# Lightning attention and a feed-forward in float32: attention steps reordered by matmul form, weights converted without GpSimd, leaky ReLU as one ScalarE operation, decay read as a Toeplitz matrix from memory

## The chip, the cores and the metric

The kernel runs on one core of one Trainium2 chip. The metric is device microseconds of one execution, the median of several runs. A core has TensorE (matmuls; PE in the profile, its weight loads PEld), VectorE (DVE), ScalarE (ACT), GpSimd (POOL) and SyncE (SP, which here only issues loads). Each takes its own instructions in order and waits for the others by semaphores. TensorE's clock is granted at one of two levels, 1.2 or 2.4 GHz; the profile shows the granted share, 1.00 being the higher.

## The reference

Batch 4, 8 heads, 768 positions, head size 64. `q` and `k`, `v` and `lam` are float32; the weights `moe_w_in` (512 x 2048) and `moe_w_out` (2048 x 512) are float64.

```python
for b in range(nb):                       # blocks of 64 positions
    intra = einsum('bhic,bhjc->bhij', qb, kb) * Dmask    # lam^(i-j) for i >= j, else 0
    intra = einsum('bhij,bhjd->bhid', intra, vb)
    inter = einsum('bhid,bhde->bhie', qb * lam_pow, kv_state)   # lam^(i+1)
    out[:, :, sl] = intra + inter
    kv_state = lam**64 * kv_state + einsum('bhsd,bhse->bhde', kb * rev_pow, vb)
x = out.transpose(0, 2, 1, 3).reshape(3072, 512)
h = x @ w_in
result = np.maximum(0.01 * h, h) @ w_out      # (3072, 512), float32
```

## The kernel before

The attention runs in 24 chunks of 128 positions, six for each batch, all heads at once, heads in pairs (one on partitions 0-63, one on 64-127). A chunk has three stages. `stage_a` loads the chunk three ahead, transposes k and q through PSUM tile `pt` (one buffer; VectorE copies kT out, ScalarE qT) and lets GpSimd make `qsT` = qT times lam^(i+1) (`pow_q`) and `kd` = k times its decay. `stage_b` forms the scores `ps` (products of 64 rows, in two halves of the array), which VectorE multiplies by `decay` into `sc`, and the state update `pu` (128 rows by 128 columns), from which VectorE makes the new `state` (L291). `stage_c` forms the output `po`: for every pair of heads one state product (L301, 128 rows by 128 columns) and then two value products (L304, 64 columns each); ScalarE copies it into `xT`. In the first chunk of a batch there is no state product, in the last no state update.

The feed-forward runs in six groups of four chunks: 16 `up` units (4 matmuls of 512 columns each, then `small` = 0.01 h on ScalarE and the maximum on VectorE, giving `gT`) and 4 `down` units (16 matmuls each). In float32 every matmul is two records in the profile, a transpose one. The stages of the next group's chunks are emitted between the units, and a scheduler then orders each engine's queue by its own model.

The weights come as 32 blocks of float64 (128 partitions x 512), loaded three ahead by SyncE, and `convert_w` rounds them on the chip: GpSimd clamps (L135) and squares (L136) the high words, VectorE works on the bits (L137, L138, L140 to L142), and GpSimd adds the low part (L143). Block n of the first 16 serves the up unit n; the last 16 serve the down units. They are converted during the first group.

The powers of lam for `decay` are made on VectorE by more than fifty small instructions (L175 to L226), `pow_q` on GpSimd.

Of the kernel before, what the change touches and what calls it, by code (L numbers as in the profile page):

```python
# [12 lines left out]
The weights come as float64, whose bits the chip rounds to float32 once, before their first use.  # L13
"""
# [28 lines left out]
def kernel(  # L43
# [35 lines left out]
    pp_t = ctx.enter_context(tc.tile_pool(name="pp_t", bufs=1, space=PS))  # L79
    pp_s = ctx.enter_context(tc.tile_pool(name="pp_s", bufs=2, space=PS))  # L80
    pp_o = ctx.enter_context(tc.tile_pool(name="pp_o", bufs=1, space=PS))
    pp_h = ctx.enter_context(tc.tile_pool(name="pp_h", bufs=2, space=PS))
    pp_y = ctx.enter_context(tc.tile_pool(name="pp_y", bufs=2, space=PS))

# [1 line left out]
    lam_b = const.tile([P, H], F32, name="lam_b")  # L86
    nc.scalar.dma_start(out=lam_b, in_=lam.partition_broadcast(P))
# [17 lines left out]
    def load_w(n):  # L105
        """The float64 bits of the n-th block: w_in for 128 features, then w_out for as many."""
# [7 lines left out]
    HI_MIN = _float_of(0x38100000)  # L114

    def convert_w(n):
        """The n-th block rounded to float32.

        A float64 is (-1)^s 2^(e-1023) (1 + m 2^-52), its high word s, e (11 bits) and the upper 20
        bits of m. While 2^-126 <= |x| < 2^128, e's upper four bits are 0111 or 1000, and the  # L120
        float32 of s, e and these 20 bits has s and e's top bit at its bits 31 and 30 and the low 27
        bits of the high word at 29-3. The low word, times 2^(e-1023-52), is then added in float32.
        Before that, magnitudes past float32 are brought down to its largest ones; what is below
        2^-126 becomes 0. Seen as float32s, the high words stand in the order of the float64s, and the
        squares of those that are left neither overflow nor underflow at these two bounds.
        """
# [11 lines left out]
        nc.vector.scalar_tensor_tensor(out=wi, in0=ti, scalar=-0x40000000, in1=wi,  # L138
                                       op0=ALU.bitwise_and, op1=ALU.bitwise_or)
# [22 lines left out]
    NR, NI = 16, C // 16 + 1  # L162
    NE = NR + NI + 1
    NB = 7
    ex = const.tile([P, NE], I32, name="ex")
    nc.gpsimd.iota(ex[:, 0:NR], pattern=[[1, NR]], base=0, channel_multiplier=-1)
    nc.gpsimd.iota(ex[:, NR:NR + NI], pattern=[[16, NI]], base=-1, channel_multiplier=-1)
    nc.gpsimd.iota(ex[:, NE - 1:NE], pattern=[[1, 1]], base=C - 1, channel_multiplier=-1)
    ir_i = const.tile([P, NR], I32, name="ir_i")
    nc.gpsimd.iota(ir_i, pattern=[[1, NR]], base=0, channel_multiplier=0)  # L170
    jr_i = const.tile([P, 1], I32, name="jr_i")
    nc.gpsimd.iota(jr_i, pattern=[[1, 1]], base=0, channel_multiplier=1)

    e_lo, e_hi = ex[:, 0:NR], ex[:, NR:NR + NI]
    nc.vector.tensor_scalar(e_lo, e_lo, 15, None, op0=ALU.bitwise_and)  # L175
    nc.vector.tensor_scalar(e_hi, e_hi, -16, None, op0=ALU.bitwise_and)
    nc.vector.tensor_scalar(jr_i, jr_i, 15, None, op0=ALU.bitwise_and)
    hi_ok = const.tile([P, NI], F32, name="hi_ok")
    nc.vector.tensor_scalar(hi_ok, e_hi, 0.0, None, op0=ALU.is_ge)
    nc.vector.tensor_scalar(e_hi, e_hi, 0.0, None, op0=ALU.max)  # L180

    ir_f = const.tile([P, NR], F32, name="ir_f")
    nc.vector.tensor_copy(ir_f, ir_i)
    jr_f = const.tile([P, 1], F32, name="jr_f")
    nc.vector.tensor_copy(jr_f, jr_i)
    same = const.tile([P, 2, NR], F32, name="same")
    nc.vector.tensor_scalar(same[:, 0, :], ir_f, jr_f[:, 0:1], None, op0=ALU.is_ge)
    nc.vector.tensor_scalar(same[:, 1, :], ir_f, jr_f[:, 0:1], None, op0=ALU.is_lt)

    bit_i = const.tile([P, NB, NE], I32, name="bit_i")  # L190
    for n in range(NB):
        nc.vector.tensor_scalar(bit_i[:, n, :], ex, n, 1, op0=ALU.arith_shift_right, op1=ALU.bitwise_and)
    bit = const.tile([P, NB, NE], F32, name="bit")
    nc.vector.tensor_copy(bit, bit_i)
    nbit = const.tile([P, NB, NE], F32, name="nbit")
    nc.vector.tensor_scalar(nbit, bit, -1.0, 1.0, op0=ALU.mult, op1=ALU.add)

    sq = const.tile([P, NB, H], F32, name="sq")
    nc.vector.tensor_copy(sq[:, 0, :], lam_b)
    for n in range(1, NB):  # L200
        nc.vector.tensor_tensor(sq[:, n, :], sq[:, n - 1, :], sq[:, n - 1, :], op=ALU.mult)

    # pw[j, h, e] = lam_h ^ ex[j, e]: the product of lam^(2^n) over the exponent's bits
    pw = const.tile([P, H, NE], F32, name="pw")
    for n in range(NB):
        f = pw if n == 0 else at2.tile([P, H, NE], F32, name="pf", tag="pf")
        nc.vector.tensor_tensor(f, _bc(bit[:, n, :], 1, H), _bc(sq[:, n, :], 2, NE), op=ALU.mult)
        nc.vector.tensor_tensor(f, f, _bc(nbit[:, n, :], 1, H), op=ALU.add)
        if n:
            nc.vector.tensor_tensor(pw, pw, f, op=ALU.mult)  # L210
    pw_hi = const.tile([P, H, NI], F32, name="pw_hi")
    nc.vector.tensor_tensor(pw_hi, pw[:, :, NR:NR + NI], _bc(hi_ok, 1, H), op=ALU.mult)
    pw_lo = const.tile([P, 2, H, NR], F32, name="pw_lo")
    for x in range(2):
        nc.vector.tensor_tensor(pw_lo[:, x], pw[:, :, 0:NR], _bc(same[:, x, :], 1, H), op=ALU.mult)
# [3 lines left out]
    decay = const.tile([P, 2, HP, C], F32, name="decay")  # L219
    for hi in range(2):  # L220
        terms = (decay[:, hi].rearrange("p a (b r) -> p a b r", r=NR),
                 at2.tile([P, HP, C], F32, name="dterm", tag="sc").rearrange("p a (b r) -> p a b r", r=NR))
        for x, dst in enumerate(terms):
# [178 lines left out]
```

## Time and profile before

| | |
|---|---|
| time, median of 3 runs | 898.42 us (898.36 to 903.91) |
| span of the profiled execution, first to last instruction | 898.1 us |
| TensorE matmul busy | 829.5 us, 2816 records |
| VectorE busy | 286.1 us, 518 instructions |
| GpSimd busy | 171.7 us, 159 instructions |
| ScalarE busy | 100.7 us, 169 instructions |
| feed-forward matmuls L322, L332 | 344.2 and 339.7 us busy, 768 records each |

The profiled execution has no time of its own beside its span, which is 0.3 us under the median. Busy times of matmuls overlap their neighbours (the mean record of 0.60 us starts every 0.43 us), so what a group of matmuls costs is read from the chain of waits, where every piece ends where the next begins.

### The profile page before, as it was taken

Reading aid. Unit: us, or ns where it says so; the run is one execution under the profiler, and the core shown is the slowest. Engines: PE = TensorE matmul, PEld = TensorE weight load, DVE = VectorE, ACT = ScalarE, POOL = GpSimd, SP = SyncE. Lnnn points to the kernel's source line nnn. Section 1 sums busy time; section 2 is a strip of 40 time slices with the busy share of each in tenths; the row PEclk is TensorE's granted clock in tenths of the full one; section 3 lists DMA queues with packets and bytes.
Section 4 is the critical chain, followed back from the end, with each engine's and each line's share of the span. In section 5 each row is a group of like instructions: output and inputs, shape, how many; then the busy total and the mean of one; then the engine's idle time right before and its main releaser. Section 6 shows DMA issues by size and latency. Waiting matters only on the chain.

```text
span 898.1 us, 7069 instructions
## 1 busy us (share of the span) xinstructions
PE 829.5 (92%) x2816; PEld 408.3 (45%) x2816; DVE 286.1 (32%) x518; ACT 100.7 (11%) x169; POOL 171.7 (19%) x159
## 2 busy tenths in 40 slices
PE   4885678759999999999999999999999999999998
PEld 3652234324455444454445454444454444444443
DVE  8789999991022220022211022111032110012000
ACT  1110101001011100011200011100011100011000
POOL 5377877771010000010010010010010000000000
PEclk9977988979999999999999999999999999999999
DMA  9354434321110102110101110111100000000000
GB/s 230 84 132 127 130 111 135 99 78 47 35 47 12 35 1 58 36 47 12 36 28 32 36 47 12 36 34 26 47 1 1 0 12 12 23 1 0 0 24 23
DMA packets 89265, 42.41 MB, mean 47 GB/s; under 512 B 75920, under 2 KB 84112, under 8 KB 89232
## 3 DMA queue, kind: packets, MB, share of 16 engines
q1 hardware_dynamic: 85632, 35.66, 15.8%
q10 hardware_dynamic: 3600, 6.30, 1.9%
q8 instruction: 22, 0.36, 0.2%
q14 instruction: 11, 0.09, 0.0%
HBM read 35.66 MB, written 6.29 MB: 47 GB/s over the span
## 4 chain that ended last, share of the span: by engine, by line
PE 79%; POOL 12%; issue 4%; DVE 4%; DMA 1%; ACT 0%; POOLq 0%; DVEq 0%
PE py L332 35%; PE ph L322 31%; POOL raw L136 4%; PE po L304 3%; PE ps L273 3%; POOL w_out L143 3%; PE po L301 3%; POOL wt L135 3%; POOL w_in L143 2%; PE pu L282 2%; PE pt L258 2%; DMA raw<-in_moe_w_in_dram 0%; DVE wt L141 0%; POOL kd L266 0%; DMA lam_b<-in_lam_dram 0%
## 5 line engine op out<-in xcount | busy, mean ns | idle before, releaser
L322 PE MATMUL ph<-xT,w_in 128*128 128x512 f32 x768 | 344.2, 602 | 16.1 <-DVE gT L326 15.3
L332 PE MATMUL py<-w_out,gT 128*128 128x512 f32 x768 | 339.7, 598 | 10.4 <-POOL w_out L143 10.4
L322 PEld LDWEIGHTS ph<-xT,w_in 128*128 128x128 f32 x768 | 144.5, 193 | 188.6 <-issue 177.6
L332 PEld LDWEIGHTS py<-w_out,gT 128*128 128x128 f32 x768 | 144.1, 191 | 183.6 <-issue 167.9
L326 DVE TENSOR_TENSOR gT<-ph,small 128x512 f32<-128x512 f32 x96 | 66.1, 689 | 240.2 <-ACT small L324 240.1
L324 ACT ACTIVATE small<-ph 128x512 f32<-128x512 f32 x96 | 57.3, 597 | 325.4 <-PE ph L322 317.1
L277 DVE TENSOR_TENSOR sc<-ps,decay 128x512 f32<-128x512 f32 x48 | 31.3, 684 | 187.4 <-PE ps L273 187.3
L266 POOL TENSOR_TENSOR kd<-k,pw 128x512 f32<-128x512 f32 x20 | 22.0, 1102 | 306.5 <-PE pu L282 224.9
L263 POOL TENSOR_TENSOR qsT<-qT,pow_q 128x512 f32<-128x512 f32 x20 | 26.0, 1299 | 217.0 <-ACT qT L260 217.0
L301 PE MATMUL po<-qsT,state 128*128 128x128 f32 x160 | 40.3, 336 | 14.7 <-DVE state L291 14.6
L260 DVE COPY kT<-pt 128x512 f32<-128x512 f32 x24 | 16.6, 690 | 109.5 <-PE pt L258 109.4
L335 ACT COPY osb<-py 128x512 f32<-128x512 f32 x24 | 14.0, 585 | 309.3 <-PE py L332 309.3
L304 PE MATMUL po<-sc,v 128*64 128x128 f32 x384 | 43.8, 315 | 5.2 <-DVE sc L277 5.2
L301 PEld LDWEIGHTS po<-qsT,state 128*128 128x128 f32 x160 | 27.1, 203 | 34.0 <-issue 18.8
L136 POOL TENSOR_TENSOR raw<-wt 128x512 f32<-128x512 f32 x32 | 41.3, 1291 | 2.5
L273 PE MATMUL ps<-qT,kT 64*128 64x128 f32 x384 | 34.2, 312 | 7.6 <-DVE sc L277 5.6
L273 PEld LDWEIGHTS ps<-qT,kT 64*128 64x128 f32 x384 | 28.5, 210 | 20.4 <-issue 11.3
L142 DVE SCALAR_TENSOR_TENSOR wt<-raw,wt 128x512 f32<-128x512 uint32 x32 | 30.5, 954 | 0.0
L304 PEld LDWEIGHTS po<-sc,v 128*64 128x64 f32 x384 | 21.3, 145 | 19.5 <-DVE sc L277 5.6
L143 POOL TENSOR_TENSOR w_out<-w_out,wt 128x512 f32<-128x512 f32 x16 | 26.0, 1624 | 18.3 <-DVE wt L142 18.3
L291 DVE SCALAR_TENSOR_TENSOR state<-state,pow_q,pu 64x64 f32<-64x64 f32 x128 | 28.3, 279 | 2.2 <-PE pu L282 1.6
L135 POOL TENSOR_SCALAR wt<-raw 128x512 f32<-128x512 f32 x32 | 27.6, 862 | 2.4
(57 smaller groups left out, 296.8 us busy)
## 6 DMA issues: line engine op xcount, KB each, us to landing
raw<-in_moe_w_in_dram SPq DMA_DIRECT2D x16, 512.0 KB, 3.8
raw<-in_moe_w_out_dram SPq DMA_DIRECT2D x16, 512.0 KB, 3.3
q<-in_q_dram SPq DMA_DIRECT2D x24, 256.0 KB, 3.8
k<-in_k_dram SPq DMA_DIRECT2D x24, 256.0 KB, 3.8
v<-in_v_dram SPq DMA_DIRECT2D x24, 256.0 KB, 3.7
out_dram<-osb ACTq DMA_DIRECT2D x24, 256.0 KB, 2.0
lam_b<-in_lam_dram ACTq DMA_DIRECT2D x1, 4.0 KB, 3.3
```

The source lines that it names most:

```text
L135: nc.gpsimd.tensor_scalar(t, hi, HI_MAX, -HI_MAX, op0=ALU.min, op1=ALU.max)
L136: nc.gpsimd.tensor_tensor(hi, t, t, op=ALU.mult)
L142: nc.vector.scalar_tensor_tensor(out=t, in0=lo, scalar=2.0 ** -52, in1=t, op0=ALU.mult, op1=ALU.mult)
L143: nc.gpsimd.tensor_tensor(w, w, t, op=ALU.add)
L273: nc.tensor.matmul(ps[hi][:, hp, :], lhsT=kT[c][HALF[hi], hp, :], rhs=qT[c][HALF[hi], hp, :], start=True, stop=True)
L277: nc.vector.tensor_tensor(sc[c][:, hi], ps[hi], decay[:, hi], op=ALU.mult)
L301: nc.tensor.matmul(po[:, hp, :], lhsT=state[(c - 1) % NST][:, hp, :], rhs=qsT[c][:, hp, :], start=True, stop=False)
L304: nc.tensor.matmul(po[HALF[hi], hp, :], lhsT=tv[:, 2 * hp + hi, :], rhs=sc[c][:, hi, hp, :], start=first, stop=True)
L322: nc.tensor.matmul(ph, lhsT=w_in_sb[f][:, ko, :], rhs=xT[g][:, ko, :], start=(ko == 0), stop=(ko == KO - 1))
L324: nc.scalar.activation(out=small, in_=ph, func=AF.Copy, bias=0.0, scale=0.01)
L326: nc.vector.tensor_tensor(t, ph, small, op=ALU.max)
L332: nc.tensor.matmul(py, lhsT=gT[f][:, ms * P:(ms + 1) * P], rhs=w_out_sb[f], start=(f == 0), stop=(f == FO - 1))
```

## The change

1. The three stages become one function `step(s)` for chunks a = s, b = s - 1 and c = s - 2, whose matmuls are emitted in groups: transposes of k, all state products of c, transposes of q, scores of b, all value products of c, state update of b. The transposes share two PSUM buffers with the state update; up and down share three.
2. `convert_w` loses its GpSimd operations. ScalarE takes the absolute value of the high words, VectorE clamps it from both sides, works on the bits and adds.
3. `up` applies the leaky ReLU by one ScalarE activation.
4. A row of 260 powers per head is built in seven doublings on 8 partitions, written 128 times to a memory table, and read back with a row step one short of the row length, which gives `decay` as a Toeplitz matrix; `pow_q` is read from the same table. Those instructions on powers go.
5. GpSimd multiplies the old state by lam^128 and VectorE adds `pu`, for all pairs at once (before: one VectorE instruction a pair of heads). The kT copy moves from VectorE to ScalarE, k is loaded before q, and the first loads and weight blocks alternate.

```diff
-    nc.scalar.dma_start(out=lam_b, in_=lam.partition_broadcast(P))
+    prow = const.tile([H, RW], F32, name="prow")        # RW = 2 * C + 4
+    nc.scalar.dma_start(out=prow[:, C + 1:C + 2], in_=lam.rearrange("(h one) -> h one", one=1))
...
+    while m < C:
+        nc.vector.tensor_scalar(prow[:, C + 1 + m:C + 1 + 2 * m], prow[:, C + 1:C + 1 + m], prow[:, C + m:C + m + 1], None,
+                                op0=ALU.mult)
+        m *= 2
+    nc.scalar.dma_start(out=toep, in_=_bc(prow[:, :], 1, C))
+    for hi in range(2):
+        nc.scalar.dma_start(out=decay[:, hi], in_=bass.AP(flat.tensor, flat.offset + hi * C * RW + C,
+                                                          [[RW - 1, P], [2 * C * RW, HP], [1, C]]))
...
-        nc.gpsimd.tensor_scalar(t, hi, HI_MAX, -HI_MAX, op0=ALU.min, op1=ALU.max)
-        nc.gpsimd.tensor_tensor(hi, t, t, op=ALU.mult)
+        nc.scalar.activation(out=t, in_=hi, func=AF.Abs)
+        nc.vector.tensor_scalar(t, t, HI_MIN, HI_MAX, op0=ALU.max, op1=ALU.min)
...
-        nc.vector.scalar_tensor_tensor(out=w, in0=hi, scalar=HI_MIN * HI_MIN, in1=w, op0=ALU.is_ge, op1=ALU.mult)
...
-        nc.gpsimd.tensor_tensor(w, w, t, op=ALU.add)
+        nc.vector.tensor_tensor(w, w, t, op=ALU.add)
...
+    def step(s):
+        a, b, c = (x if 0 <= x < NCH else None for x in (s, s - 1, s - 2))
+        if a is not None:
...
+            kT[a] = transposed(loaded[a][0], "kT", 2)
...
+        if c is not None:
+            po = pp_o.tile([P, HP, C], F32, name="po", tag="po")
+            inter = c % NCB > 0
+            if inter:
+                for hp in range(HP):
+                    nc.tensor.matmul(po[:, hp, :], lhsT=state[(c - 1) % NST][:, hp, :], rhs=qsT[c][:, hp, :],
+                                     start=(hp == 0), stop=False, skip_group_check=True)
+        if a is not None:
+            qT[a] = transposed(loaded[a][1], "qT", 2)
...
+                nc.gpsimd.tensor_tensor(new[z], state[(b - 1) % NST][z], _bc(lam_c[HALF[hi]], 2, D), op=ALU.mult)
+                nc.vector.tensor_tensor(new[z], new[z], pu[z], op=ALU.add)
...
-        nc.scalar.activation(out=small, in_=ph, func=AF.Copy, bias=0.0, scale=0.01)
-        nc.vector.tensor_tensor(t, ph, small, op=ALU.max)
+        nc.scalar.activation(out=t, in_=ph, func=AF.Prelu, bias=0.0, scale=1.0, alpha=0.01)
```

TensorE's queue, before, around a chunk between down and up units (py is a down unit's PSUM tile, ph an up unit's; the transposes stand earlier, between down matmuls):

```order
L332 MATMUL py<-w_out_127,gT_1124 128x512
L301 MATMUL po<-qsT,state_249 128x128
L304 MATMUL po<-sc,v 64x128 x2
L301 MATMUL po<-qsT,state_249 128x128
L304 MATMUL po<-sc,v 64x128 x2
L301 MATMUL po<-qsT,state_249 128x128
L304 MATMUL po<-sc,v 64x128 x2
L301 MATMUL po<-qsT,state_249 128x128
L304 MATMUL po<-sc,v 64x128 x2
L273 MATMUL ps<-qT,kT 128x128 x8
L282 MATMUL pu<-v,kd 128x128 x4
L322 MATMUL ph<-xT,w_in_96 128x512 x4
```

and now, at the same place:

```order
L284 MATMUL py<-w_out_143,gT_1012 128x512
L203 MATMUL pt<-ident,k 128x128 x4
L225 MATMUL po<-qsT,state_174 128x128 x4
L203 MATMUL pt<-ident,q 128x128 x4
L237 MATMUL ps<-qT,kT 128x128 x8
L247 MATMUL po<-sc,v 64x128 x8
L258 MATMUL pu<-v,kd 128x128 x4
L276 MATMUL ph<-xT,w_in_112 128x512 x4
```

All matmuls of a step now stand in one block, each kind in one piece. VectorE's queue in the conversion of w_out, before (wt is the scratch tile, raw the float64 bits):

```order
L141 TENSOR_SCALAR wt<-w_out_113 128x512
L137 TENSOR_SCALAR w_out_114<-wt 128x512
L142 SCALAR_TENSOR_TENSOR wt<-raw,wt 128x512
L138 SCALAR_TENSOR_TENSOR w_out_114<-wt,w_out_114 128x512
L277 TENSOR_TENSOR sc<-ps,decay 128x512
L140 SCALAR_TENSOR_TENSOR w_out_114<-raw,w_out_114 128x512
```

and now:

```order
L168 SCALAR_TENSOR_TENSOR wt<-raw,wt 128x512
L163 TENSOR_SCALAR wt<-wt 128x512
L169 TENSOR_TENSOR w_out_137<-w_out_137,wt 128x512
L164 TENSOR_SCALAR w_out_138<-wt 128x512
L241 TENSOR_TENSOR sc<-ps,decay 128x512
L165 SCALAR_TENSOR_TENSOR w_out_138<-raw,w_out_138 128x512
L163 TENSOR_SCALAR wt<-wt 128x512
```

A block now has six VectorE instructions, three with one input (L163, L164, L167) and three with two (L165, L168, L169), where five stood beside three of GpSimd. ScalarE's queue at the start, now (toep is the table in memory, prow the row of powers):

```order
L94 DMA prow<-in_lam_dram 8x1
L101 DMA toep<-prow 1024x1x260
L205 ACT_TABLE_LOAD
L205 COPY kT<-pt 128x512
L106 DMA decay<-toep 128x4x128 x2
L111 DMA pow_q<-toep 64x4x128 x2
L205 COPY qT<-pt 128x512
L205 COPY kT<-pt 128x512
L162 ACTIVATE wt<-raw 128x512
```

The copies of qT and kT stand behind four reads that wait for the table; before, ScalarE issued one load there and then copied. The one table load of its activation functions is the only one in the queue, as before.

## Rows read from the trace of the kernel before

**Rows 1.** The page, part 2: granted clock in 40 slices, in tenths.

```profile
PEclk9977988979999999999999999999999999999999
```

**Rows 2.** Busy time by stretch: stretch, length, engines (instructions), clock, DMA share, GB/s.

```profile
0.00:25.00 25.00, 9.38 (x45) 7.19 (x45) 20.61 (x57) 2.45 (x3) 14.60 (x31) 1.00 1.08 220
50.00:203.00 153.00, 106.74 (x326) 50.55 (x326) 137.86 (x192) 13.45 (x23) 114.95 (x94) 0.84 0.39 115
204.00:894.00 690.00, 689.32 (x2294) 332.40 (x2293) 108.27 (x230) 81.12 (x137) 31.38 (x27) 1.00 0.09 24
```

**Rows 3.** GpSimd's timeline: start us, us, engine, line; in brackets its wait before.

```profile
139.82 0.70 POOL L135 TENSOR_SCALAR wt<-raw 128x512 f32<-128x512 f32 x1
140.60 1.27 POOL L136 TENSOR_TENSOR raw<-wt 128x512 f32<-128x512 f32 x1
142.50 1.65 POOL L143 TENSOR_TENSOR w_out<-w_out,wt 128x512 f32<-128x512 f32 x1 [0.63 <-DVE wt L142]
...
157.56 1.64 POOL L143 TENSOR_TENSOR w_out<-w_out,wt 128x512 f32<-128x512 f32 x1 [0.63 <-DVE wt L142]
```

**Rows 4.** The chain of waits, pieces: start us, us, engine, line, records.

```profile
203.81 13.14 PE py L332 x30
...
839.53 54.95 PE py L332 x128
...
894.50 0.59 ACT osb L335
```

**Rows 5.** The chain, one full chunk between down matmuls.

```profile
467.22 0.44 PE pt L258 x4
467.66 0.86 PE py L332 x2
468.52 0.58 PE pt L258 x4
...
481.97 0.22 PE po L301 x2
482.19 0.37 PE po L304 x4
482.56 0.42 PE po L301 x2
...
484.93 1.09 PE ps L273 x16
486.02 1.09 PE pu L282 x8
```

**Rows 6.** The chain, value products of a batch's first chunk.

```profile
405.96 1.02 PE po L304 x16
```

**Rows 7.** VectorE's conversion lines: duration ns min/median/max, first and last start.

```profile
L141 DVE TENSOR_SCALAR wt<-w_out x16: 411/904/1265, 125.5 to 200.2; 128x512 int32<-128x512 int32 x16
L142 DVE SCALAR_TENSOR_TENSOR wt<-raw,wt x32: 676/680/1530, 38.7 to 201.7; 128x512 f32<-128x512 uint32 x32
```

**Rows 8.** Groups by line: busy us, mean ns of one, idle before, releaser.

```profile
L326 DVE TENSOR_TENSOR gT<-ph,small 128x512 f32<-128x512 f32 x96 | 66.1, 689 | 240.2 <-ACT small L324 240.1
L324 ACT ACTIVATE small<-ph 128x512 f32<-128x512 f32 x96 | 57.3, 597 | 325.4 <-PE ph L322 317.1 <-DVE w_in L138 5.0 <-DVE w_out L138 3.2
```

**Rows 9.** The chain, first pieces.

```profile
0.74 3.29 DMA lam_b<-in_lam_dram
...
4.26 0.18 DVE sq L201
```

**Rows 10.** DMA issues of the first 30 us: count, KB each, median us to landing.

```profile
k<-in_k_dram SPq DMA_DIRECT2D x5, 256.0 KB, 5.0
```

**Rows 11.** TensorE's timeline: the first up unit, and one after a hole.

```profile
62.99 7.03 PE L322 MATMUL ph<-xT,w_in 128*128 128x512 f32 x16
...
113.63 5.21 PE L322 MATMUL ph<-xT,w_in 128*128 128x512 f32 x8 [5.59 <-DVE gT L326]
```

More of the change, by code (lines that the diff above doesn't have):

```diff
@@ L78 @@
     PS = bass.MemoryType.PSUM
[L79 removed]
+    pp_t = ctx.enter_context(tc.tile_pool(name="pp_t", bufs=2, space=PS))
     pp_s = ctx.enter_context(tc.tile_pool(name="pp_s", bufs=2, space=PS))
     pp_o = ctx.enter_context(tc.tile_pool(name="pp_o", bufs=1, space=PS))
[L82 to L87 removed]
+    pp_f = ctx.enter_context(tc.tile_pool(name="pp_f", bufs=3, space=PS))
+    dram = ctx.enter_context(tc.tile_pool(name="dram", bufs=1, space=bass.MemoryType.DRAM))
+    RW = 2 * C + 4
+    prow = const.tile([H, RW], F32, name="prow")
+    nc.vector.memset(prow, 0.0)
+    nc.vector.memset(prow[:, C:C + 1], 1.0)
+    nc.scalar.dma_start(out=prow[:, C + 1:C + 2], in_=lam.rearrange("(h one) -> h one", one=1))
+    m = 1
+    while m < C:
+        nc.vector.tensor_scalar(prow[:, C + 1 + m:C + 1 + 2 * m], prow[:, C + 1:C + 1 + m], prow[:, C + m:C + m + 1], None,
+                                op0=ALU.mult)
+        m *= 2
+    toep = dram.tile([H, C, RW], F32, name="toep")
+    nc.scalar.dma_start(out=toep, in_=_bc(prow[:, :], 1, C))
+    decay = const.tile([P, 2, HP, C], F32, name="decay")
+    flat = toep[:, :, :]
+    for hi in range(2):
+        nc.scalar.dma_start(out=decay[:, hi], in_=bass.AP(flat.tensor, flat.offset + hi * C * RW + C,
+                                                          [[RW - 1, P], [2 * C * RW, HP], [1, C]]))
+    pow_q = const.tile([P, HP, C], F32, name="pow_q")
+    for hi in range(2):
+        nc.scalar.dma_start(out=pow_q[HALF[hi]], in_=bass.AP(flat.tensor, flat.offset + hi * C * RW + C + 1,
+                                                             [[RW, D], [2 * C * RW, HP], [1, C]]))
     loaded = {}
@@ L147 @@
     AHEAD = 3
-    for c in range(AHEAD):
-        load(c)
     W_AHEAD = 3
-    for n in range(W_AHEAD):
-        load_w(n)
+    load(0)
+    load_w(0)
+    load(1)
+    load_w(1)
+    load(2)
+    load_w(2)
     ident = const.tile([P, P], F32, name="ident")
     make_identity(nc, ident)
[L162 to L223, printed above, removed]
-            nc.vector.tensor_tensor(
-                dst, _bc(pw_lo[:, x, hi::2, :], 2, NI - 1), _bc(pw_hi[:, hi::2, 1 - x:NI - x], 3, NR), op=ALU.mult)
-        nc.vector.tensor_tensor(terms[0], terms[0], terms[1], op=ALU.add)
@@ L229 @@
-    pow_q = const.tile([P, HP, C], F32, name="pow_q")
-    for hi in range(2):
-        nc.gpsimd.tensor_copy(pow_q[HALF[hi], :, 0], lam_b[HALF[hi], hi::2])
-    m = 1
-    while m < C:
-        nc.gpsimd.tensor_tensor(pow_q[:, :, m:2 * m], pow_q[:, :, 0:m], _bc(pow_q[:, :, m - 1], 2, m), op=ALU.mult)
-        m *= 2
-    pow_k = pw[:, :, NE - 1]
+    pow_k = decay[:, :, :, C - 1].rearrange("p hi hp -> p hp hi")
+    lam_c = pow_q[:, :, C - 1]
     NST = 3
@@ L249, in pair @@
         return t[:, 2 * hp:2 * hp + 2, :].rearrange("p a d -> p (a d)")
-    def stage_a(c):
-        if c + AHEAD < NCH:
-            load(c + AHEAD)
-        tq, tk, _ = loaded[c]
-        for src, d, nm, bufs in ((tk, kT, "kT", 2), (tq, qT, "qT", 3)):
-            pt = pp_t.tile([P, HP, C], F32, name="pt", tag="pt")
-            for hp in range(HP):
-                nc.tensor.transpose(out=pt[:, hp, :], in_=pair(src, hp), identity=ident)
-            d[c] = at3.tile([P, HP, C], F32, name=nm, tag=nm, bufs=bufs)
-            (nc.vector.tensor_copy if nm == "kT" else nc.scalar.copy)(d[c], pt)
-        if c % NCB:
-            qsT[c] = at3.tile([P, HP, C], F32, name="qsT", tag="qsT")
-            nc.gpsimd.tensor_tensor(qsT[c], qT[c], pow_q, op=ALU.mult)
-        if c % NCB < NCB - 1:
-            kd[c] = at2.tile([P, H, D], F32, name="kd", tag="kd")
-            nc.gpsimd.tensor_tensor(kd[c], tk, _bc(pow_k, 2, D), op=ALU.mult)
@@ L268, in stage_b @@
-    def stage_b(c):
-        ps = [pp_s.tile([P, HP, C], F32, name="ps", tag="ps") for _ in range(2)]
-        for hp in range(HP):
-            for hi in range(2):
-                nc.tensor.matmul(ps[hi][:, hp, :], lhsT=kT[c][HALF[hi], hp, :], rhs=qT[c][HALF[hi], hp, :],
-                                 start=True, stop=True)
-        sc[c] = at2.tile([P, 2, HP, C], F32, name="sc", tag="sc")
-        for hi in range(2):
-            nc.vector.tensor_tensor(sc[c][:, hi], ps[hi], decay[:, hi], op=ALU.mult)
-        if c % NCB == NCB - 1:
-            return
-        pu = pp_o.tile([P, HP, P], F32, name="pu", tag="po")
-        for hp in range(HP):
-            nc.tensor.matmul(pu[:, hp, :], lhsT=pair(kd[c], hp), rhs=pair(loaded[c][2], hp), start=True, stop=True)
-        new = state[c % NST]
-        for hi in range(2):
-            z = (HALF[hi], slice(None), HALF[hi])
-            if c % NCB == 0:
-                nc.vector.tensor_copy(new[z], pu[z])
-                continue
-            for hp in range(HP):
-                z = (HALF[hi], hp, HALF[hi])
-                nc.vector.scalar_tensor_tensor(out=new[z], in0=state[(c - 1) % NST][z], scalar=pow_q[HALF[hi], hp, C - 1:C],
-                                               in1=pu[z], op0=ALU.mult, op1=ALU.add)
@@ L294, in stage_c @@
-    def stage_c(c):
-        g, off = c // CPG, (c % CPG) * C
-        first = c % NCB == 0
-        tv = loaded[c][2]
-        po = pp_o.tile([P, HP, C], F32, name="po", tag="po")
-        for hp in range(HP):
-            if not first:
-                nc.tensor.matmul(po[:, hp, :], lhsT=state[(c - 1) % NST][:, hp, :], rhs=qsT[c][:, hp, :],
-                                 start=True, stop=False)
-            for hi in range(2):
-                nc.tensor.matmul(po[HALF[hi], hp, :], lhsT=tv[:, 2 * hp + hi, :], rhs=sc[c][:, hi, hp, :],
-                                 start=first, stop=True)
-        if g not in xT:
-            xT[g] = xp.tile([P, KO, MS], F32, name="xT", tag="xT")
-        nc.scalar.copy(out=xT[g][:, :, off:off + C], in_=po)
-        del loaded[c]
@@ L311, with transposed @@
-    steps = []
-    for s in range(NCH + 2):
-        for fn, c in ((stage_c, s - 2), (stage_b, s - 1), (stage_a, s)):
-            if 0 <= c < NCH:
-                steps.append((fn, c))
-    ends = [steps.index((stage_c, g * CPG + CPG - 1)) + 1 for g in range(NG)]
+    def transposed(src, nm, bufs):
+        pt = pp_t.tile([P, HP, C], F32, name="pt", tag="pt")
+        for hp in range(HP):
+            nc.tensor.transpose(out=pt[:, hp, :], in_=pair(src, hp), identity=ident)
+        t = at3.tile([P, HP, C], F32, name=nm, tag=nm, bufs=bufs)
+        nc.scalar.copy(t, pt)
+        return t
@@ L319, in up @@
+    NSTEP = NCH + 2
+    ends = [g * CPG + CPG + 2 for g in range(NG)]
     def up(g, f, gT):
-        ph = pp_h.tile([P, MS], F32, name="ph", tag="ph")
+        ph = pp_f.tile([P, MS], F32, name="ph", tag="ff")
         for ko in range(KO):
             nc.tensor.matmul(ph, lhsT=w_in_sb[f][:, ko, :], rhs=xT[g][:, ko, :], start=(ko == 0), stop=(ko == KO - 1))
-        small = tp.tile([P, MS], F32, name="small", tag="small")
-        nc.scalar.activation(out=small, in_=ph, func=AF.Copy, bias=0.0, scale=0.01)
@@ L343, in attend @@
         while at < upto:
-            steps[at][0](steps[at][1])
+            step(at)
             at += 1
@@ L362 @@
         total = sum(u[2] for u in units)
-        begin, end = at, ends[g + 1] if g + 1 < NG else len(steps)
+        begin, end = at, ends[g + 1] if g + 1 < NG else NSTEP
         done = 0
```

49 lines of the change are left out of this document (44 added, 5 removed).

## The prediction

> **What bounds the kernel now.** I read the page first, then the busy time by stretch, then the chain of waits inside each stretch, and last the durations that the new work will have.
>
> The clock line of the page [rows 1] shows dips in the first quarter and full speed from then on. The stretches say why [rows 2]. From 204 to 894 us TensorE is busy for 689 of 690 us at a granted clock of 1.00: nothing but fewer or cheaper matmuls can shorten that. From 50 to 203 us it is busy for 107 of 153 us at 0.84, while GpSimd is busy for 115 us and VectorE for 138 us. There the rows of GpSimd's own timeline [rows 3] set the pace: for each weight block it clamps, squares, waits for VectorE's tail of the conversion and adds. From the add at 142.50 to the one at 157.56, three blocks take 15.06 us, so 5.0 us a block, and 32 blocks are 160 us. The first w_out block must be converted before the first down projection, the last one before its end; the stretch ends at 203.81, when the down matmuls run without a hole [rows 4].
>
> So there are two stages: one of 204 us at the pace of the conversion, and one of 694 us at the pace of TensorE. The profiled execution has a span of 898.1 us; the median of the three runs shown is 898.42, so 0.3 us lies around the span. My sum is made in the span and I add nothing.
>
> **The change, part by part.**
>
> *TensorE, fixed part.* The feed-forward is untouched: 1536 matmul records. 128 of them take 54.95 us [rows 4], 0.4293 us each, so 659.4 us in all. Behind the last lie 3.6 us of copy and store (894.50 to 898.1); they stay.
>
> *TensorE, attention.* Before, a full chunk between down matmuls costs [rows 5]: transposes 0.44 + 0.58; then state and value products in turn, 0.22 + 4 x 0.37 + 3 x 0.42 = 2.96; scores 1.09; state update 1.09: 6.16 us. The price is in the alternation: a chunk whose value products stand alone takes 1.02 for the sixteen [rows 6], where four by four they take 1.48, and the state products, 0.22 a pair right after the feed-forward, take 0.42 a pair after a value product. In the new order each kind stands alone: 0.44 + 4 x 0.22 (0.88) + 0.44 + 1.09 + 1.02 + 1.09 = 4.96. A change of form from scores to value products has no row of its own; it lies between nothing and the 0.20 that a state pair loses. I take 0.05, so 5.0 us; both ends go into the range. Everything that a step reads was made a step earlier, except that the state update now reuses the transposes' bank: it needs ScalarE's copy of kT, which is due some 0.6 us after the first 0.44 us of a 5 us step, so I cost it at nothing.
>
> *The conversion.* GpSimd's three operations go (0.7 to 1.65 us each [rows 3]). VectorE gets six a block: three with one input and three with two. The same kinds took 0.41 at best and 0.90 in the median with GpSimd running beside them, and 0.68 [rows 7]. With GpSimd nearly idle I take the former: 3 x 0.41 + 3 x 0.68 = 3.27 us a block; the other end is 3 x 0.90 + 3 x 0.68 = 4.74. The absolute value goes to ScalarE: about the 0.60 of its 128x512 pass [rows 8], hidden beside VectorE.
>
> *The leaky ReLU.* VectorE's 0.69 us goes and ScalarE's 0.60 us becomes another operation on the same tile [rows 8]. Its own duration is not in the trace. An up unit needs 8 x 0.4293 = 3.43 us on TensorE, so anything up to that is hidden; I cost it at nothing.
>
> *The start.* Decay now comes through memory, in series: lam lands in 3.3 us [rows 9] behind two short fills, say at 4.5; seven products at 0.2 from start to start make 5.9; then the table of 8 x 128 x 260 x 4 bytes, 1.06 MB, is written while the first loads keep the queues at 220 GB/s [rows 2]: 4.8 us if it had all of that, some 9 us at half; then a read like a 256 KB load, 5.0 us [rows 10]. Decay is there at about 20 us, between 16 and 30. ScalarE issues these reads in order, so the first qT copy stands behind the table write; the chain of the attention starts with decay all the same. Six further steps are needed before the first up unit. A step is 5.0 us of TensorE at full clock and up to twice that at half; with loads three chunks ahead and VectorE converting between, I take 5.7: 20 + 34 = 54 us. The lower end is 46; the upper is the 63 us at which the first up unit starts now [rows 11], with one more step at half clock, 73.
>
> The first slices' rows show one queue of loads over all engines at 220 GB/s, which gives the table 5 to 9 us. The Trainium skill's page "DMA: Bandwidth & Descriptors" (Rules for kernel authors) says that a transfer whose outermost dimension is smaller than 16 is spread over no more engines than that dimension; the table write's is 8, so by the page it would take up to twice as long and the sum would be up to 9 us more. No row of this trace shows such a transfer; the late start below covers its price.
>
> *Does the conversion then keep up?* By 54 us five blocks are converted, as far as the order of VectorE's queue goes. TensorE wants the last w_out block after 16 up units (55 us), two steps (10) and 22 rows of the interleaved down matmuls (19): 84 us later. VectorE needs 27 x 3.27 = 88 us and about 4 us for scores and states: late by 8 us. At 2.95 us a block, with starts a little closer than durations, it would not be late. I take 4 us.
>
> *The sum.* First up unit at 54. From there 659.4 of feed-forward. Steps 7 to 25 hold 17 pairs of transposes (15.0), 16 sets of state products (14.1), 18 of scores (19.6), 19 of value products (19.4) and 15 state updates (16.4): 84.5, with 0.05 to 0.1 a change of form 86. Wait for weights 4, tail 3.6. Together **807 us**, 91 less than now. Of these about 19 come from the order by form (the same steps at the old prices: 105) and the rest from the conversion stage.
>
> **The rivals.**
>
> *Late start, 826 us.* The table write or ScalarE's queue holds the attention back to the upper end, 73 us: 807 + 19. For it: nothing in the trace shows such a write. 10%.
>
> *Order by form gains nothing, 826 us.* The cost of a change of form shows up between any two groups: 807 + 19. Against it: sixteen value products in one piece did run at 1.02 [rows 6]. 7%.
>
> *VectorE becomes the bound, 851 us.* At 4.74 a block it needs 128 + 4 = 132 us, 48 later than wanted: 807 - 4 + 48. For it: the median of 0.90 [rows 7]; against it: GpSimd, beside which that median arose, has little left. 7%.
>
> *The clock falls at every step, 923 us, slower.* Transposes, small products and score products now stand in one block of 5 us. If the granted clock dropped to the half level (1.2 of 2.4 GHz) there, each of 17 steps would cost 5.0 more, and the feed-forward behind it 1.8 (eight records took 5.21 us after a hole of 5.59 [rows 11], where 3.43 is normal): 17 x 6.8 = 116 and 807 + 116. It decides from 91 / 17 = 5.4 us a step. Against it: transposes inside the feed-forward run at 0.11 each and the row behind them at full rate [rows 5], clock 1.00 throughout [rows 2]. 2%. The Trainium skill's page "TensorE: Matmul & The Clock Gate" (Part 4: PE-mode transpose) says that transposes do not count as busy time for the clock gate; by that rule this rival is possible, and the trace so far does not bear it out, since 0.88 us of transposes never cost the clock.
>
> That the change doesn't do what it says I count with the second rival: the instruction order shows whole groups, and only their price can disappoint.
>
> **How the numbers follow.** The forecast has 70%, its own range 794 to 820 (start 46 to 62, step 4.95 to 5.2, wait 0 to 8). With the two rivals at 826 and their spread, **793 to 832** holds about eight in ten; the 851, the 923 and a still better start are left out. About 1% (9 us) is what a measurement of this kernel can tell from no change. Every case but the last lies more than 5% below 898: faster 0.96, same 0.02, slower 0.02.
>
> **What would show it.** Right: a first up unit near 54 us; the first down unit ending near 150 us with GpSimd hardly busy; VectorE at 3 to 3.3 us a block; a full step in 5.0 us between feed-forward rows, first transposes to end of state update; granted clock 1.00 from about 60 us on. Wrong: feed-forward waiting for w_out beyond 10 us (VectorE or ScalarE's queue), a step above 5.5 us, a decay read that lands after 30 us, or ScalarE's new pass above 3.4 us.

## The result, and the profile after

The changed kernel takes **837.15 us** in the median of four runs (835.13 to 837.89), against 900.5 for the kernel before beside it: a ratio of 0.9295, interval 0.9262 to 0.9327. That is 30 us above the forecast of 807, and 5 us above the end of the range. The profiled execution has a span of 835.7 us.

The page of the changed kernel: its first line, the busy times (part 1) and the granted clock (part 2).

```profile
span 835.7 us, 6817 instructions
...
PE 783.0 (94%) x2816; PEld 397.5 (48%) x2816; DVE 155.3 (19%) x289; ACT 132.3 (16%) x225; POOL 74.2 (9%) x81
...
PEclk9999999999999999999999999999999999999999
```

The dips of [rows 1] are gone. TensorE is still idle for 53 of 836 us. Its timeline (start, us, and in brackets the wait ahead) shows most of this ahead of the first up unit, which starts 12 us later than before [rows 11], 7.9 us in three waits, and the rest behind the last matmul:

```profile
74.94 27.73 PE L276 MATMUL ph<-xT,w_in 128*128 128x512 f32 x64
...
142.37 1.20 PE L258 MATMUL pu<-v,kd 128*128 128x128 f32 x8 [4.20 <-issue]
143.36 11.28 PE L284 MATMUL py<-w_out,gT 128*128 128x512 f32 x22
155.54 1.98 PE L284 MATMUL py<-w_out,gT 128*128 128x512 f32 x4 [0.90 <-DVE w_out L169]
160.30 18.27 PE L284 MATMUL py<-w_out,gT 128*128 128x512 f32 x38 [2.77 <-DVE w_out L169]
```

The busy time by stretch (stretch, length, engines, granted clock, DMA share, GB/s) shows the conversion stage, the rest, and the short pieces behind the three waits:

```profile
75.00:165.00 90.00, 82.12 (x266) 39.57 (x266) 86.50 (x169) 30.00 (x50) 12.14 (x8) 0.96 0.58 173
165.00:832.00 667.00, 666.71 (x2248) 329.08 (x2246) 34.39 (x63) 87.29 (x151) 40.19 (x44) 1.00 0.09 24
...
142.40:147.00 4.60, 4.60 (x13) 2.50 (x14) 4.57 (x6) 0.97 (x3) 2.90 (x2) 0.63 0.85 229
...
155.54:157.60 2.06, 1.98 (x4) 0.68 (x4) 2.00 (x4) 0.68 (x1) 1.82 (x2) 1.00 0.76 255
...
160.30:164.00 3.70, 3.70 (x5) 1.65 (x6) 3.63 (x9) 1.33 (x2) 0.00 (x0) 0.54 0.34 131
```

Before, TensorE worked without a hole from 204 us on [rows 2]; now it does from 165 us on. What the start looks like, the chain of waits tells (start, us, what): the wait for decay, one step of the attention, and one of three waits for a transpose buffer with what runs behind it.

```profile
12.29 20.29 DMA k<-in_k_dram
...
32.60 7.71 DMA decay<-toep
...
40.49 1.07 POOL kd L217
...
49.99 0.44 PE pt L203 x4
50.43 0.89 PE po L225 x8
51.32 0.44 PE pt L203 x4
51.76 1.09 PE ps L237 x16
52.85 1.02 PE po L247 x16
53.87 1.09 PE pu L258 x8
...
56.29 3.20 issue
59.49 0.63 PE pt L203 x4
60.11 1.09 PE ps L237 x16
```

The chain puts the time up to 32.58 down to a load of k. ScalarE's own timeline names the other candidate:

```profile
5.78 0.84 ACTq L101 DMA_DIRECT2D toep<-prow  x1
...
7.94 0.59 ACT L205 COPY kT<-pt 128x512 f32<-128x512 f32 x1
31.84 1.21 ACTq L106 DMA_DIRECT2D decay<-toep  x2
...
35.44 0.58 ACT L205 COPY qT<-pt 128x512 f32<-128x512 f32 x1 [26.92 <-DMA decay<-toep]
```

The table write is issued at 5.78; the reads behind it go out at 31.84, 26 us later, and the first qT copy stands behind them. Decay lands at 40.3 where the prediction had 20. Against the sum of 807 the profiled span stands as follows (us):

| term | predicted | measured |
|---|---|---|
| first up unit | 54 | 74.9 |
| feed-forward, 1536 x 0.4293 | 659.4 | 659.4 (at the same price: 128 records take 54.93 and 54.95 at the end) |
| attention steps behind it | 86 | 84.6 (the same counts at 0.88, 0.89, 1.09, 1.02, 1.09 a group) |
| waits of TensorE | 4 | 7.9 (4.20 + 0.90 + 2.77) |
| clock behind these waits | 0 | 3.9 |
| tail | 3.6 | 3.9 |
| rest | | 1.1 |

The 3.9 of clock are worked out: the 64 down records between 143.36 and the next step at 178.41 have 35.05 us; without the two waits between them 31.4, where 64 x 0.4293 are 27.5. The granted clock of the two slow pieces accounts for 4.6 x 0.37 + 3.7 x 0.46 = 3.4 of them.

### The profile page after: what moved, and what is told of

Same layout as the page of the kernel before. It is cut to its first block, busy times and chain, and to the rows that moved or that the text cites. A ratio compares the mean times of both kernels' runs of the same rounds, so it can differ in the third digit from the quotient of the medians.

```text
span 835.7 us, 6817 instructions
## 1 busy us (share of the span) xinstructions
PE 783.0 (94%) x2816; PEld 397.5 (48%) x2816; DVE 155.3 (19%) x289; ACT 132.3 (16%) x225; POOL 74.2 (9%) x81
## 4 chain that ended last, share of the span: by engine, by line
PE 85%; DVE 7%; DMA 4%; issue 2%; SPq 1%; ACT 0%; POOL 0%; POOLq 0%; ACTq 0%
PE py L284 38%; PE ph L276 34%; PE ps L237 3%; PE po L247 3%; PE pu L258 2%; DMA k<-in_k_dram 2%; PE pt L203 2%; PE po L225 2%; DVE wt L168 2%; DVE w_out L165 1%; DVE wt L163 1%; DMA decay<-toep 1%; DVE wt L167 1%; SPq L135 1%; SPq L122 1%
## 5 line engine op out<-in xcount | busy, mean ns | idle before, releaser
L278 ACT ACTIVATE gT<-ph 128x512 f32<-128x512 f32 x96 | 57.0, 595 | 242.9 <-PE ph L276 242.9
L231 POOL TENSOR_TENSOR qsT<-qT,pow_q 128x512 f32<-128x512 f32 x20 | 25.8, 1290 | 478.3 <-ACT qT L205 459.4
L203 PE MATMUL pt<-ident,q 128*128 128x128 f32 x96 | 16.0, 294 | 31.7 <-ACT qT L205 25.9
L258 PE MATMUL pu<-v,kd 128*128 128x128 f32 x160 | 24.1, 296 | 6.6 <-issue 4.2
L162 ACT ACTIVATE wt<-raw 128x512 f32<-128x512 f32 x32 | 21.7, 679 | 50.4 <-DVE w_out L169 28.3
L266 POOL TENSOR_TENSOR state<-state,pow_q 64x256 f32<-64x256 f32 x32 | 25.1, 785 | 24.6 <-DVE state L267 13.9
L217 POOL TENSOR_TENSOR kd<-k,decay 128x512 f32<-128x512 f32 x20 | 21.8, 1091 | 55.3 <-DMA decay<-toep 37.8
L247 PE MATMUL po<-sc,v 128*64 128x128 f32 x384 | 26.3, 279 | 0.0
L258 PEld LDWEIGHTS pu<-v,kd 128*128 128x128 f32 x160 | 20.2, 198 | 10.2 <-issue 7.3
L168 DVE SCALAR_TENSOR_TENSOR wt<-raw,wt 128x512 f32<-128x512 uint32 x32 | 24.6, 770 | 0.4
L203 PE MATMUL pt<-ident,k 128*128 128x128 f32 x96 | 15.8, 292 | 6.7 <-DMA k<-in_k_dram 6.7
L163 DVE TENSOR_SCALAR wt<-wt 128x512 f32<-128x512 f32 x32 | 15.5, 484 | 33.9 <-ACT wt L162 33.9
```

What stands on the lines that cost most here:

```text
L163: nc.vector.tensor_scalar(t, t, HI_MIN, HI_MAX, op0=ALU.max, op1=ALU.min)
L203: nc.tensor.transpose(out=pt[:, hp, :], in_=pair(src, hp), identity=ident)
L231: nc.gpsimd.tensor_tensor(qsT[a], qT[a], pow_q, op=ALU.mult)
L247: nc.tensor.matmul(po[HALF[hi], hp, :], lhsT=tv[:, 2 * hp + hi, :], rhs=sc[c][:, hi, hp, :], start=(not inter and hp == 0), stop=True, ski ...
L258: nc.tensor.matmul(pu[:, hp, :], lhsT=pair(kd[b], hp), rhs=pair(loaded[b][2], hp), start=(hp == 0), stop=True, skip_group_check=True)
L266: nc.gpsimd.tensor_tensor(new[z], state[(b - 1) % NST][z], _bc(lam_c[HALF[hi]], 2, D), op=ALU.mult)
```

## The experiments

All are edits of the changed kernel. Runs of the kernel before lay between 898.0 and 903.9 us, so ratios tell more than differences of a few us.

| run | median us | ratio to before | first up unit at |
|---|---|---|---|
| changed kernel | 837.15 | 0.9295 (0.9262 to 0.9327) | 74.9 |
| row on 16 partitions | 829.43 | 0.9206 (0.9173 to 0.9240) | 69.2 |
| row on 128 partitions | 811.32 | 0.9022 (0.8983 to 0.9061) | 51.7 |
| row of 1280 bytes | 839.36 | 0.9322 (0.9269 to 0.9375) | 77.0 |
| first loads held back | 837.32 | 0.9299 (0.9253 to 0.9346) | 77.9 |
| powers as before | 816.40 | 0.9037 (0.9002 to 0.9071) | 56.3 |
| products in turn again | 859.56 | 0.9516 (0.9479 to 0.9553) | 81.7 |
| conversion as before | 896.17 | 0.9935 (0.9913 to 0.9957) | 145.8 |
| bank for the state update | 837.89 | 0.9288 (0.9263 to 0.9314) | 74.7 |
| leaky ReLU as before | 835.19 | 0.9266 (0.9239 to 0.9294) | 74.6 |
| 128 partitions and bank | **809.79** | 0.8984 (0.8959 to 0.9009) | 51.8 |
| the same, deeper buffers | 812.46 | 0.9008 (0.8983 to 0.9034) | 57.6 |
| 128 partitions, loads held back | 818.79 (one run) | | 59.4 |

**Is it the table at all?** Powers, decay and `pow_q` are made on the chip as before; all else is as changed.

```diff
-    nc.scalar.dma_start(out=toep, in_=_bc(prow[:, :], 1, C))
...
+    lam_b = const.tile([P, H], F32, name="lam_b")
+    nc.scalar.dma_start(out=lam_b, in_=lam.partition_broadcast(P))
```

> The changed kernel with the powers of lam made on VectorE and GpSimd as before (no table in memory). If the late decay is what the prediction missed: decay near 26 us in place of 40, first up unit near 61 in place of 74.9, total 823 (14 less). If something else holds the start (loads, the shared bank, the clock): first up unit stays above 70, total 834 or more.

816.4 us, 20.8 less than the changed kernel, with the first up unit 18.6 earlier; 14 were expected of both. The start through memory costs what the first term of the sum missed.

**Why the write takes 26 us.** Three theories: contention with the first loads, rows of 1040 bytes, or the 8 partitions from which it reads. The first run holds the first loads back until decay is there; the second makes the rows 1280 bytes; the third and fourth lay the row on 16 and on 128 partitions (NP), 64 and 8 copies from each. A load is held back by a copy from `decay` into the tile that it fills. A mask, not shown, gives each of the NR partitions of a head its lam.

```diff
+            if c < 3:
+                nc.gpsimd.tensor_copy(x[:, 0, 0:1], decay[:, 1, 0, 0:1])
...
+        if n < 3:
+            nc.gpsimd.tensor_copy(w_raw[n].bitcast(F32)[:, 0:1], decay[:, 1, 0, 0:1])
```

```diff
-    RW = 2 * C + 4
+    RW = 320
```

```diff
-    prow = const.tile([H, RW], F32, name="prow")
+    prow = const.tile([NP, RW], F32, name="prow")
...
-    nc.scalar.dma_start(out=toep, in_=_bc(prow[:, :], 1, C))
+    nc.scalar.dma_start(out=toep.rearrange("h (r j) w -> (h r) j w", r=NR), in_=_bc(prow[:, :], 1, C // NR))
```

> The loads of the first three chunks and of the first three weight blocks wait until decay has been read, so that the table write and its reads have the queues to themselves. Theory C (contention): the write takes 5 us, decay is there near 15 us. Theories A and B: the write still takes 20 us or more, and the loads that come after it are added: first up unit past 80, total 843 or more.

> Rows of 320 elements (1280 bytes, a multiple of 256) in place of 260 (1040 bytes); still 8 partitions, 23% more bytes. Theory D (rows that don't fill whole lines of memory cost more): write under 12 us, total 822 or less. Theories A and B: write as long as before or 23% longer, 26 to 32 us, total 837 to 843.

> The row of powers on 16 partitions (two a head, each writing 64 copies) in place of 8 (each 128 copies); same bytes, same rows. In the changed kernel the table write holds about half of the DMA engines from 5.8 to 31.8 us. Theory A (the outermost dimension of 8 confines the write to 8 engines, at some 190 ns a row on each): 16 engines, 64 rows each, write over in 12 to 14 us, first up unit near 62 instead of 74.9, total 824. Theory B (one source partition at a time gives so little): the same here. Theory C (the write only waits behind the first loads): no change, 837. Theory D (rows of 1040 bytes are slow by their length): no change in the bytes' price a row, but more engines: like A.

> The row of powers on all 128 partitions (16 a head, each writing 8 copies). Theory A (number of engines): as with 16 partitions, write 12 to 14 us, total 824. Theory B (reads from one source partition are slow): clearly shorter than with 16 partitions, 5 to 8 us, first up unit near 55, total 817. Theory C (contention with the first loads): no change, 837.

Held back, the loads leave the write alone, and the chain of that kernel still shows 24.9 us for it; the read behind it takes 3.6 instead of 7.7:

```profile
5.53 24.88 DMA toep<-prow
...
30.87 3.56 DMA decay<-toep
```

The DMA view of its first 40 us, one figure a microsecond (busy share of 16 engines in tenths, and GB/s), shows the write at 47 GB/s with four tenths of the engines' time busy:

```profile
DMA  0090000444444444444444444444420299619999
GB/s 0 17 226 19 0 0 0 50 49 46 48 48 47 47 47 48 46 48 47 48 48 47 47 47 47 47 47 49 45 26 0 37 295 311 143 33 221 272 221 257
```

So contention is out as the main cause. It also shows that the load of k in the chain was no cause: with the loads moved away the write takes as long. Longer rows make it longer (29.7 us for 1.23 times the bytes), so the row's length is out too. The DMA issues of the other two (last column: us from issue to landing), 16 partitions first:

```profile
toep<-prow ACTq DMA_DIRECT2D x1, 1040.0 KB, 13.3
```

```profile
toep<-prow ACTq DMA_DIRECT2D x1, 1040.0 KB, 8.5
```

26 us, 13.3, 8.5: the partitions decide. With 16 only 5.7 us came through to the first up unit, since ScalarE issued the decay read at 26.87, behind an absolute value that waited for a weight load until 26.79. With 128, 23 us came through, and 25.8 in the total.

**Engines or partitions?** 16 engines at the rate that 8 showed would move 94 GB/s. The last of this group has 128 partitions and the loads held back.

> The first loads wait for decay, as in the earlier run with 8 partitions, and the row of powers stands on 128 partitions, so the write of 1.06 MB is alone on the queues. Rates by engine: 8 engines moved 47 GB/s, so 16 move 94 and the write takes 11 to 12 us. Rates by source partition: it takes less than the 8.5 us that it took beside the loads, down to 5 us at 220 GB/s. The total, since the loads start later, 812 to 820 in either case.

Its chain, and its DMA view as above:

```profile
6.33 5.84 DMA toep<-prow
...
12.62 3.61 DMA decay<-toep
```

```profile
DMA  0074000399800499529999999999999999999898
GB/s 0 4 162 100 0 0 0 131 350 348 232 3 0 80 343 257 107 54 255 240 203 295 330 246 217 219 263 330 256 217 218 248 339 262 219 226 222 147 219 198
```

5.84 us from issue to landing, 4.3 times as fast as from 8 partitions, where the count of engines alone would give 2. While the bytes move, nine tenths of the engines' time are busy in place of four, and the rate is 350 GB/s in place of 47, seven times. So spreading the source over partitions counts beyond the number of engines: 8 of them gave 5.9 GB/s each. Whether the partition sets that, a group of neighbouring partitions, an engine that reads from a single partition row after row, or the order in which the rows reach memory, no run tells apart. The total is 7.5 us worse than with free loads, since these come late.

**The order by form.** State products stand before the two value products of their pair again.

```diff
-            if inter:
-                for hp in range(HP):
-                    nc.tensor.matmul(po[:, hp, :], lhsT=state[(c - 1) % NST][:, hp, :], rhs=qsT[c][:, hp, :],
-                                     start=(hp == 0), stop=False, skip_group_check=True)
...
             for hp in range(HP):
+                if inter:
+                    nc.tensor.matmul(po[:, hp, :], lhsT=state[(c - 1) % NST][:, hp, :], rhs=qsT[c][:, hp, :],
+                                     start=(hp == 0), stop=False, skip_group_check=True)
                 for hi in range(2):
```

> The changed kernel with each pair's state product put back in front of its two value products; everything else as changed. By the prediction's prices a step with state products costs 2.96 + 0.2 in place of 0.88 + 1.02 there, 1.06 to 1.26 us more, 20 times: total 858 to 862. If the order by form gains nothing: 837.

859.56, 22.4 more, 6.7 of them ahead of the first up unit. The chain of that kernel shows the old prices of [rows 5] inside the new step, 6.2 us in all in place of 4.97:

```profile
219.68 0.42 PE po L243 x2
220.10 0.37 PE po L246 x4
220.47 0.42 PE po L243 x2
220.89 0.37 PE po L246 x4
```

**The conversion with GpSimd again.**

```diff
-        nc.scalar.activation(out=t, in_=hi, func=AF.Abs)
-        nc.vector.tensor_scalar(t, t, HI_MIN, HI_MAX, op0=ALU.max, op1=ALU.min)
+        nc.gpsimd.tensor_scalar(t, hi, HI_MAX, -HI_MAX, op0=ALU.min, op1=ALU.max)
+        nc.gpsimd.tensor_tensor(hi, t, t, op=ALU.mult)
...
-        nc.vector.tensor_tensor(w, w, t, op=ALU.add)
+        nc.gpsimd.tensor_tensor(w, w, t, op=ALU.add)
```

> The changed kernel with the conversion as before (GpSimd clamps, squares and adds). If GpSimd's 5.0 us a block was the bound of the first stage: 32 blocks take 160 us from about 40 us on, down units run freely from 200 us in place of 160, total 875 to 880. If the pace of the first stage has another cause (loads, start): 845 or less.

896.17, 16 to 21 more than expected. TensorE's timeline shows the two longest waits and the first up unit:

```profile
84.44 1.11 PE L204 MATMUL pt<-ident,q 128*128 128x128 f32 x4 [74.18 <-ACT qT L206]
...
106.93 2.08 PE L259 MATMUL pu<-v,kd 128*128 128x128 f32 x8 [19.36 <-POOL kd L218]
...
145.79 4.57 PE L277 MATMUL ph<-xT,w_in 128*128 128x512 f32 x10
```

The first wait is ScalarE's: its qT copy stands behind the four reads of the table, which go out from 68.58 to 83.76 here (decay's at 31.84 in the changed kernel); the profile puts its 75.00 us of waiting down to a load of weights, which no run tests. The second is GpSimd's: the first `kd` starts at 105.82 in its queue, behind half of the conversion (40.49 in the changed kernel). So the up units come after that half instead of beside it: 145.8 + 659.4 + 85 + 4 = 894. Both the pace and the queues are changed here, so the run doesn't price the pace alone.

**The bank of the state update, and the leaky ReLU**, which the prediction costed at nothing.

```diff
-    pp_f = ctx.enter_context(tc.tile_pool(name="pp_f", bufs=3, space=PS))
+    pp_f = ctx.enter_context(tc.tile_pool(name="pp_f", bufs=2, space=PS))
+    pp_u = ctx.enter_context(tc.tile_pool(name="pp_u", bufs=1, space=PS))
...
-            pu = pp_t.tile([P, HP, P], F32, name="pu", tag="pt")
+            pu = pp_u.tile([P, HP, P], F32, name="pu", tag="pu")
```

```diff
-        nc.scalar.activation(out=t, in_=ph, func=AF.Prelu, bias=0.0, scale=1.0, alpha=0.01)
+        nc.scalar.activation(out=small, in_=ph, func=AF.Copy, bias=0.0, scale=0.01)
+        nc.vector.tensor_tensor(t, ph, small, op=ALU.max)
```

> The changed kernel with a PSUM bank of its own for the state update, which no longer shares the two of the transposes (up and down share two in place of three). In the changed kernel TensorE stands 3.2 + 1.4 + 1.0 us before transposes of q and 4.2 us before one state update. Theory P (the shared bank makes TensorE wait for ScalarE's and VectorE's queues): these 9.8 us go, total 827. Theory Q: they go, but the 4.2 come back as waiting for w_out, total 831. Theory R (the waits are for something else): no change, 837.

> The changed kernel with the leaky ReLU as two operations again (0.01 h on ScalarE, the maximum on VectorE). The prediction's own reason: an up unit has 3.43 us on TensorE, so 0.60 + 0.69 us are hidden and the total stays at 837 to 840. Rival: between the first up unit and the last converted block VectorE and TensorE are both nearly full, so the 16 maxima of the first group, 0.69 us each, push the conversion back by 11 us and the total goes to 845 to 849, with the wait for w_out longer by as much.

837.89: no change. The waits for the bank (4.20, and 5.65 at the start) are gone, and TensorE waits elsewhere, as its timeline in that kernel shows:

```profile
57.70 2.67 PE L238 MATMUL ps<-qT,kT 64*128 64x128 f32 x16 [3.04 <-DVE sc L242]
...
117.16 3.70 PE L277 MATMUL ph<-xT,w_in 128*128 128x512 f32 x8 [2.90 <-ACT gT L279]
...
160.80 14.55 PE L285 MATMUL py<-w_out,gT 128*128 128x512 f32 x30 [2.77 <-DVE w_out L170]
```

The last starts within 0.5 us of where it starts with the shared bank: the queues of the conversion set it. The run also takes one of three buffers from up and down, and TensorE waits there for ScalarE to read an up tile (2.90 above); what the bank is worth without that, no run shows. And 835.19 for the old leaky ReLU: no loss, the rival of 845 to 849 is wrong. Half of that rival did happen: with the 16 maxima in VectorE's queue its last w_out block starts its last operation at 174.34 instead of 167.25. But TensorE waits only 6.0 us in that stage (4.09 + 1.61 + 0.28) where the changed kernel waits 7.9. Its queue is in another order there: parts of a later step stand between the last down matmuls (171.96 to 180.77), and so they are not waited for. The new operation gains nothing here.

**The best version.** 128 partitions and the bank together; then with three scratch tiles instead of two and five weight blocks loaded ahead instead of three.

> The row of powers on 128 partitions, and a PSUM bank of its own for the state update. Theory: with the early start the wait of 3.1 us of the state update for its bank is the largest one left in front of the weights, but the conversion still sets when the last block is ready, so 809 to 812, no more than 2 us off the 811.3 with the wide row alone. Rival: the early start took the conversion out of the limit, and the 3.1 us come off: 807 to 809.

> As the last, with three scratch tiles in place of two and five blocks of float64 loaded ahead in place of three. ScalarE's absolute value waits 29 us in all for VectorE to free a scratch tile in the stretch 50 to 200 with the wide row, and VectorE waits 4.2 us for ScalarE. Theory: VectorE alone is the pace (2.94 us a block), so deeper buffers give back only its few us of waiting: 807 to 810. Rival: more loads at the start take the queues from the chunks' loads and the first up unit comes 2 to 5 us later: 812 to 816.

809.79, a tenth below the kernel before and 3.3% below the changed one. Against 128 partitions alone it is 1.5 us less, within their intervals. Its timeline has 4.3 us of waits left:

```profile
102.48 10.57 PE L287 MATMUL ph<-xT,w_in 128*128 128x512 f32 x24 [0.82 <-ACT gT L289]
124.37 1.13 PE L295 MATMUL py<-w_out,gT 128*128 128x512 f32 x2 [1.23 <-DVE w_out L180]
127.78 23.25 PE L295 MATMUL py<-w_out,gT 128*128 128x512 f32 x48 [2.28 <-DVE w_out L180]
```

Deeper buffers don't help: the first up unit comes 5.9 us later and the total is 812.46, as the rival had it (812 to 816, by 2 to 5 us). That the added loads are the cause, no further run shows.

## Why the prediction was wrong

**The step that failed** is the price of the table: "Decay is there at about 20 us, between 16 and 30". The write was priced at 4.8 to 9 us from the 220 GB/s of the first slices, a rate of loads that end on 128 partitions. This write starts from 8 and took 26 us; with nothing beside it, it took 24.9. The read behind it, 7.7 for 5.0, added a little. Decay came at 40.3, past the 30 that the prediction had named as a sign of being wrong, and the first up unit came 20.9 us late.

The sentence on the Trainium skill's page "DMA: Bandwidth & Descriptors" (Rules for kernel authors) pointed the right way: an outermost dimension of 8 keeps a transfer on at most 8 engines. The trace agrees, with a busy share of 0.4 to 0.5 of 16 engines. By the prediction's estimate from that page the write would have taken up to 18 us; it took 26, so the rule is a part of the price: from 128 partitions the gain was 4.3 and not 2.

**The rival named "late start"** named the table write and had, by chance, nearly the right start (73 us against 74.9): the 73 is a step at half clock added to the old start, not a price of the write. It gave 826 because it left the rest of the sum as it was.

**The wait for weights**, 4, was 7.9. 4.2 of it is the state update waiting for a bank, "due some 0.6 us after the first 0.44": ScalarE copied kT only at 141.69, behind a leaky ReLU and an absolute value, which had waited 1.40 us for a load. The prediction looked at when the copy is due, not at what stands ahead of it. Freed from the bank, TensorE waits about as long elsewhere, since the conversion decides: from the first up unit to the end of the last block it took 93.0 us (74.94 to 167.94), where the prediction had 88 + 4 against the 84 at which TensorE wants it. By its own sum VectorE was 8 us late, and it took 4; 8 would have been nearer. ScalarE's timeline in front of that state update:

```profile
140.65 0.66 ACT L162 ACTIVATE wt<-raw 128x512 f32<-128x512 f32 x1 [1.40 <-DMA raw<-in_moe_w_out_dram]
...
141.69 0.58 ACT L205 COPY kT<-pt 128x512 f32<-128x512 f32 x1
```

**The clock** behind these waits cost 3.4 to 3.9 us and has no term in the sum, though row 113.63 [rows 11] had shown the effect behind a longer hole, and the fourth rival used it.

**Right**: the six steps of the start in their sum (34.6 us from decay to the first up unit, predicted 34), though partly by luck: full steps there take 4.97 and not 5.7, and 5.65 us are waits for a transpose buffer, which the prediction put at nothing; the step of 4.97 us, at 102.51 to 107.48; the order by form (1.23 us a step, so 19.7 for the 16 steps with state products behind the first up unit, predicted 19; 22.4 in the whole kernel); VectorE's pace: four finished blocks in its timeline, two by two 5.88 us apart, so 2.94 a block (predicted 3.27, with 2.95 as the other case), and 3.35 on average over the 26 blocks from 80.09 to 167.25 with the attention's work between (predicted 92 / 27 = 3.41), with one-input operations at 0.45 on average, near the 0.41 taken and not at the median of 0.90 [rows 7];

```profile
131.98 0.69 DVE L169 TENSOR_TENSOR w_out<-w_out,wt 128x512 f32<-128x512 f32 x1
133.98 0.68 DVE L169 TENSOR_TENSOR w_out<-w_out,wt 128x512 f32<-128x512 f32 x1
137.86 0.69 DVE L169 TENSOR_TENSOR w_out<-w_out,wt 128x512 f32<-128x512 f32 x1
139.86 0.69 DVE L169 TENSOR_TENSOR w_out<-w_out,wt 128x512 f32<-128x512 f32 x1
```

and ScalarE's new pass, in the page at the 0.60 of the old one [rows 8]:

```profile
L278 ACT ACTIVATE gT<-ph 128x512 f32<-128x512 f32 x96 | 57.0, 595 | 242.9 <-PE ph L276 242.9
```

The clock did not fall at the steps: 1.00 from 165 to 832 us, with steps of 0.88 us of transposes in it. The rule of the Trainium skill's page "TensorE: Matmul & The Clock Gate" (Part 4: PE-mode transpose), that a transpose doesn't count as busy in the same way, has no price that shows in these steps.

Of the 63 us gained (900.5 against 837.15), the order by form is worth 22, the table -21, the leaky ReLU nothing. If the parts add up, the remaining 62 or so belong to the conversion and the other edits; no run shows them alone, as the run with the old conversion, 59 us slower, also has the late reads of the table.

## What to carry to other kernels

Price a transfer by a row that has the same shape on both sides: how many partitions it reads from and writes to, not only its bytes. A constant that goes through memory is in series with everything that needs it, so spread its source over all partitions before counting on it. And where two engines share a stage, a wait that is removed comes back at the next queue until the slowest one moves.

## What the runs showed of the hardware

A write to memory of 1.06 MB took 24.9 us from 8 partitions and 5.84 from 128, each alone on the queues; beside loads 26, 13.3 (16 partitions) and 8.5. And the granted clock gave way behind some short waits of TensorE: 0.63 in the 4.6 us behind a wait of 4.20 and 0.54 in the 3.7 us behind one of 2.77, while the piece between them, behind a wait of 0.90, ran at 1.00. The length of the wait alone doesn't decide: behind the wait of 3.20 at 56.29 the clock stayed at 1.00 (scores at 1.09, as in a full step), and behind the 2.90 in the run with the bank too (eight up records in 3.70 us, where they took 5.21 behind the hole of [rows 11]).
